# Attention in turns of three key tiles instead of two, with its slot plan laid anew, ahead of two MLPs on one core

## The chip, the core and the metric

The kernel runs on one core of a Trainium2 chip. The metric is the time of one execution on the device in microseconds (us), the median of several. The core has a matrix engine (TensorE, PE in the rows; its weight loads are PEld), a vector engine (DVE), a scalar engine (ACT), GpSimd (POOL) and a queue engine (SP) that issues most transfers. Each engine runs its own instructions strictly in the order in which the program issued them.

## The reference

Three layers, one after the other. The first is attention with B=2, H=8, S=768, D=64, in which a query sees only the keys of its own cluster:

```
q_assign = argmax(normalised q . normalised centroids)      # 16 clusters, k_assign alike
scores = where(q_assign == k_assign, q k^T / sqrt(D), -1e9)
attn = exp(scores - max(scores)); attn = attn / (sum(attn) + 1e-9)
x = (attn v) as [1536, 512]
```

The second is h = x w_in (512 to 2048), g = max(h, 0) + alpha min(h, 0), x = g w_out. The third is an RMS norm, then (silu(xn w_gate) * (xn w_val)) w_out with 1536 inner columns. Everything is float32.

## The kernel before

**Phases, slots and turns.** Heads are worked in eight pairs. A pair has two phases, one for each half of its queries (384 columns), so there are 16 phases, numbered 0 to 15. A phase has six slots, one for each key tile of 128 keys, which makes 96 slots. In a slot the two heads of the pair each get a score tile (`st_tile`, two matmuls L642 and L643 into one of three one-bank PSUM buffers `ps_st`; the exponential on ACT at L644 writes one half of a buffer `p`, of which there are four). Every second slot has a turn (`pv_tiles`): the exponentials of two key tiles against the values (L658, float32, two heads side by side in 64 columns of the array each) and against ones for the softmax's sums (L672, 32 columns each, four side by side), both into the two-bank buffer `ps_pv`. In phases 4 to 12 (`SUMMED`) DVE first adds the `p` of two tiles (L663), and only the last turn of the phase has sums, of the adds and of the last two tiles.

**Maxima.** A slot also holds one max tile (`max_tile`, two matmuls L595 into the one two-bank buffer `ps_mx`, reduced on DVE at L599), for a phase nine slots ahead (`LEAD`; phases 0 to 3 have slots of their own in `AHEAD`). When a head's three tiles are reduced, `max_split` (DVE L604, L605) cuts the maximum in two parts, `max_rows` (PE L620, into the single buffer `ps_pr`) turns them into rows, and `rows_copy` (ACT L629) puts these into the operand of the score matmuls.

**Ends of phases.** `out_evac` (ACT L680) takes sums and values out of `ps_pv`, `out_sums` (PE L687) and `out_recip` (DVE L692, L693) make the reciprocals, `out_bcast` (PE L701) spreads them, `out_mult` (DVE L707) multiplies, and `out_split` (ACT L715, POOL L718) cuts the result into the two parts that the first MLP reads. L687, L701, L620, the cluster products (L458, L469) and the transposed one-hot rows (L516) all share `ps_pr`.

**Work for later pairs.** Loads, squares (ACT L411), norms (DVE), high and low parts (ACT L548, DVE or POOL L556), cluster products, argmax and one-hot rows of the pairs ahead stand in the tables `PAIR`, `FOURTH`, `THIRD`, `SECOND`. From slot 70 on the packed weights of the first MLP are decoded (`decode_step`; the tables `EARLY` and `TAIL` place the steps).

**What sets the order.** `plan()` lists every such step with a slot and an order number within the slot; `slot()` issues the steps of a slot by that number. The number is all that decides what an engine does first:

```
def slot(self, s):
    for _, _, fn, a in sorted(self.ev.pop(s, []), key=lambda x: x[:2]):
        fn(*a)
```

Behind the last slots come the two MLPs, all of whose matmuls stand at L919.

## Time and profile before

| | |
|---|---|
| three runs | 857.28, 857.35, 857.57 us; median 857.35 |
| the profiled execution | 859.05 us, its span 857.3 us |
| granted TensorE clock over the span | 0.998 of full speed |
| instructions in the span | 11501 |

The span is what the profiler sees between the first and the last instruction; the profiled execution lies 1.7 us above the median. In the rows, L with a number is a line of the kernel, `out<-in` are buffers, and xN counts instructions. A float32 matmul leaves two records, so four value matmuls stand as x8. The end of a matmul is modelled and overlaps the start of the next, so paces are read from start to start.

### The profile page before, as it was taken

The page shows a single profiled execution, that of the slowest core. Times are in us where ns is not written, and L with a number is a line of the kernel's source. Part 1 is how long each engine was busy: PE and PEld are TensorE (multiplying, and loading weights), DVE is VectorE, ACT ScalarE, POOL GpSimd, SP SyncE. Part 2 cuts the span into 40 slices and gives each one's busy share as a digit, 9 for nine tenths or more (in the row PEclk, how much of TensorE's full clock was granted, in tenths as well). Part 3 has the DMA queues.
Part 4 walks back from the last instruction along what each step waited for, and adds up shares of the span by engine and source line. Part 5 has one row for each costly group of instructions (what it writes and reads, how often), then busy time and mean ns, then how long its engine had stood idle before and what let it go on. Part 6 is the DMA issues. An engine that isn't in the chain of part 4 may idle for free.

```text
span 857.3 us, 11501 instructions
## 1 busy us (share of the span) xinstructions
PE 835.6 (97%) x4310; PEld 632.4 (74%) x4310; DVE 596.7 (70%) x904; ACT 330.9 (39%) x636; POOL 376.2 (44%) x323
## 2 busy tenths in 40 slices
PE   8999999999999999999999999999999999999998
PEld 5555666666556688887788888778888888888886
DVE  7778687776767439999889786887645545555523
ACT  6636555655545333333334344533222212222210
POOL 3420211221004427878777664444546455555511
PEclk9999999999999999999999999999999999999999
DMA  8776447625632002222222211001122121121012
GB/s 204 193 213 168 99 129 197 124 74 129 138 99 99 25 1 73 99 74 99 75 74 74 74 50 49 24 26 34 66 74 65 58 74 53 71 74 50 1 49 99
DMA packets 23623, 74.02 MB, mean 86 GB/s; under 512 B 3600, under 2 KB 4752, under 8 KB 23568
## 3 DMA queue, kind: packets, MB, share of 16 engines
q1 hardware_dynamic: 23568, 73.29, 29.6%
q8 instruction: 34, 0.56, 0.3%
q14 instruction: 21, 0.17, 0.1%
HBM read 49.88 MB, written 3.15 MB: 62 GB/s over the span
## 4 chain that ended last, share of the span: by engine, by line
PE 72%; DVE 18%; issue 3%; ACT 2%; DMA 1%; POOL 1%; SPq 0%; DVEq 0%; ACTq 0%; POOLq 0%
PE ps_st L919 24%; PE ps_mx L919 10%; PE ps_pv L919 10%; PE ps_pv L658 7%; PE ps_pr L919 5%; PE ps_mx L595 4%; DVE mx L599 4%; DVE dec_a L898 3%; PE ps_pv L672 3%; PE ps_st L642 3%; PE ps_st L643 3%; DVE x L1026 2%; DVE dec_a L896 2%; PE ps_pr L701 1%; DVE dec_e L901 1%
## 5 line engine op out<-in xcount | busy, mean ns | idle before, releaser
L982 POOL TENSOR_TENSOR gl<-v,gh 128x512 fp32r<-128x512 f32 x68 | 93.5, 1375 | 104.0 <-ACT gh L981 102.6
L644 ACT ACTIVATE p<-ps_st 128x384 f32<-128x384 f32 x192 | 85.1, 494 | 105.6 <-PE ps_st L643 104.9
L599 DVE TENSOR_REDUCE mx<-ps_mx 128x1 f32<-128x768 f32 x92 | 87.7, 954 | 42.6 <-PE ps_mx L595 41.9
L981 ACT CAST gh<-v 128x512 fp32r<-128x512 f32 x68 | 42.3, 622 | 134.1 <-DVE v L978 79.9
L978 DVE TENSOR_TENSOR v<-ps_st,t 128x512 f32<-128x512 f32 x36 | 24.9, 691 | 85.5 <-PE ps_st L919 85.5
L718 POOL TENSOR_TENSOR x1l<-X,x1h 128x384 fp32r<-128x384 f32 x15 | 16.0, 1065 | 148.5 <-ACT x1h L715 111.6
L658 PE MATMUL ps_pv<-p,vnat 128*64 128x384 f32 x384 | 74.0, 507 | 0.2 <-DVE mx L599 0.2
L974 DVE SCALAR_TENSOR_TENSOR v<-v,alpha,t 128x512 f32<-128x512 f32 x45 | 46.7, 1037 | 30.9 <-ACT v L973 30.9
L919 PE MATMUL ps_st<-x1h,stage 128*128 128x512 f32 x272 | 67.8, 390 | 0.0
L642 PE MATMUL ps_st<-op 128*128 128x384 f32 x192 | 67.5, 351 | 0.3 <-ACT p L644 0.3
L898 DVE SCALAR_TENSOR_TENSOR dec_a<-raw,dec_a 128x512 uint32<-128x512 uint32 x66 | 66.1, 1001 | 2.3
L1026 DVE TENSOR_TENSOR x<-ps_mx,x 128x1024 f32<-128x1024 f32 x36 | 43.8, 1218 | 31.1 <-PE ps_mx L919 31.1
L643 PE MATMUL ps_st<-op 82*128 82x384 f32 x192 | 65.0, 339 | 0.1
L595 PE MATMUL ps_mx<-op 80*128 80x384 f32 x184 | 55.3, 382 | 8.5 <-DVE mx L599 7.4
L906 POOL TENSOR_TENSOR dec_a<-dec_a,woh 128x512 f32<-128x512 f32 x28 | 45.4, 1623 | 36.1 <-ACT woh L909 32.3
L919 PEld LDWEIGHTS ps_st<-x1h,stage 128*128 128x128 f32 x272 | 50.9, 188 | 10.6 <-ACT x1h L1068 0.2
L595 PEld LDWEIGHTS ps_mx<-op 80*128 80x128 f32 x184 | 27.9, 188 | 38.7 <-DVE mx L599 17.9
L919 PE MATMUL ps_st<-x1h,wvh 128*128 128x512 f32 x144 | 56.1, 390 | 0.0
L919 PE MATMUL ps_st<-x1h,wvl 128*128 128x512 f32 x144 | 56.1, 390 | 0.0
L919 PE MATMUL ps_st<-x1h,wih 128*128 128x512 f32 x132 | 51.7, 392 | 0.0
L919 PE MATMUL ps_st<-x1h,wil 128*128 128x512 f32 x132 | 51.5, 390 | 0.0
L901 DVE TENSOR_SCALAR dec_e<-dec_a 128x512 uint32<-128x512 uint32 x66 | 48.7, 737 | 2.2
(282 smaller groups left out, 1969.9 us busy)
## 6 DMA issues: line engine op xcount, KB each, us to landing
raw<-in_moe_w_out_dram SPq DMA_DIRECT2D x28, 512.0 KB, 3.5
op<-stage SPq DMA_DIRECT2D x32, 384.0 KB, 5.7
raw<-in_moe_w_in_dram SPq DMA_DIRECT2D x15, 512.0 KB, 3.6
raw<-in_moe_w_val_dram SPq DMA_DIRECT2D x12, 512.0 KB, 3.4
raw<-in_moe_w_gate_dram SPq DMA_DIRECT2D x12, 512.0 KB, 3.4
op<-stage SPq DMA_DIRECT2D x16, 288.0 KB, 5.8
raw<-in_qt_dram SPq DMA_DIRECT2D x8, 384.0 KB, 4.5
raw<-in_kt_dram SPq DMA_DIRECT2D x8, 384.0 KB, 5.4
```

Of the source, the lines that this page charges most:

```text
L595: nc.tensor.matmul(ps[:, g, :self.HS], lhsT=o1[0:80, 0, t * 128:(t + 1) * 128], rhs=o1[0:80, 1, sl], start=True, stop=True)
L599: nc.vector.tensor_reduce(out=self.mx[ph][:, k:k + 1], in_=ps[:, :, :self.HS], op=ALU.max, axis=AX.XY)
L642: nc.tensor.matmul(ps, lhsT=o1[:, 1, ks], rhs=o1[:, 0, qs], start=True, stop=False)
L643: nc.tensor.matmul(ps, lhsT=o2[:, 1, ks], rhs=o2[:, 0, qs], start=False, stop=True)
L644: nc.scalar.activation(out=self.P[s][:, e], in_=ps, func=AF.Exp, scale=self.scale)
L658: nc.tensor.matmul(ps[64 * e:64 * e + 64], lhsT=self.vnat[ph // 2][:, e, t0 + y], rhs=P[y][:, e], start=t0 + y == 0, stop=t0 + y == T - 1)
L898: v.scalar_tensor_tensor(out=a, in0=top, scalar=0xC0000000, in1=a, op0=ALU.bitwise_and, op1=ALU.bitwise_or)
L901: v.tensor_scalar(out=e, in0=a, scalar1=0xFF800000, scalar2=None, op0=ALU.bitwise_and)
L919: self.nc.tensor.matmul(ps, lhsT=a, rhs=b, start=first and i == 0, stop=last and i == len(terms) - 1)
L974: nc.vector.scalar_tensor_tensor(out=v, in0=v, scalar=self.nalpha[:, a], in1=t, op0=ALU.mult, op1=ALU.add)
L982: nc.gpsimd.tensor_tensor(out=lo, in0=v, in1=f(hi), op=ALU.subtract)
L1026: nc.vector.tensor_tensor(out=dst, in0=ps, in1=dst, op=ALU.add)
```

## The change

A turn now takes three key tiles, and there are two of them in a phase, in the third and the sixth slot, in the same slot as their last key tile (before: three turns of two tiles, each in the slot after). The values' matmuls stay twelve a phase. The sums are now made in each turn: in the phases of `SUMMED` four matmuls, of the sum of the first two tiles (one add a turn, in a function of its own, `pv_add`) and of the third; in phases 0 to 3 and 13 to 15 six, four for the first two tiles and two for the third.

The max tile of the second slot of each phase now goes to `ps_pv` instead of `ps_mx` (the argument `aside`); the order number of a max tile follows from its slot modulo 3. Phases 2 and 3 have other slots for their max tiles, and `max_rows` and `rows_copy` of later phases come one slot later. The ends of phases come earlier: from phase 2 on the evacuation at the end of the phase's last slot, then `out_sums` in the next, `out_bcast` two and `out_split` three slots behind that slot (before: eight, ten and twelve slots behind the phase's first). The pairs' table is laid anew. The weights' decode is cut into seven steps of one instruction, with ACT's copy moved ahead of two of DVE's, and its steps have new places.

```
-            for t in range(T):
...
-                if t % 2:
-                    at(b + t + 1, 2, self.pv_tiles, (b + t) // 2)
-            calm = STEADY <= b + 7 and not last
-            at(b + (7 if calm else 6), 1.03 if calm else 3, self.out_evac, ph)
-            at(b + (7 if last else 8), -0.5 if last else 1.7, self.out_sums, ph)
-            at(b + (8 if last else 10), -0.3 if last else 2.2, self.out_bcast, ph)
+                if t % 3 == 2:
+                    if ph in SUMMED:
+                        at(b + t, 0.9, self.pv_add, b + t - 2)
+                    at(b + t, 2, self.pv_tiles, b + t - 2)
+            at(b + 5, 2.9, self.out_evac, ph)
+            x, y, z = (7, 8, 8) if last else (8, 10, 12) if ph < 2 else (6, 8, 9)
+            at(b + x, -0.5 if last else 1.7, self.out_sums, ph)
+            at(b + y, -0.3 if last else 2.2, self.out_bcast, ph)
...
-                early = s < 0 or s % 2 and (s > 15 or ph < DIRECT and (s == 15 or slots.count(s) > 1))
-                at(s, 2.7 if s in slots[:k] else 0.5 if early else 1.5 if s < STEADY else 1.01, self.max_tile, ph, k)
+                second = s in slots[:k]
+                o = 2.7 if second else 0.5 if s < 0 else (0.5, 1.01, 1.03)[s % 3]
+                if s >= 0 and s % 3 == 0 and s - 1 in DOUBLE:
+                    o = 1.03
+                aside = not k % 2 if s < 0 else s % T == 1 and not second
+                at(s, o, self.max_tile, ph, k, aside)
...
-                at(end, 1.45 if end % 2 and end > 0 else 1.6, self.max_split, ph, 1)
+                at(end, 2.75 if end == slots[-2] else 1.6, self.max_split, ph, 1)
                 at(end + 1, 0.7, self.max_rows, ph, 1)
...
-                at(end + 1, 0.7, self.max_rows, ph, None)
-                at(end + 1, 1.03, self.rows_copy, ph)
+                at(end + 2, 1.7, self.max_rows, ph, None)
+                at(end + 2, 1.71, self.rows_copy, ph)
...
+    def pv_add(self, s):
+        a = self.pre([128, 2, self.HS], f"add{s % self.T // 3}")
+        self.adds[s] = a
+        self.nc.vector.tensor_tensor(out=a, in0=self.P[s], in1=self.P[s + 1], op=ALU.add)
...
+        def total(q, y, start, stop):
+            r = 32 * (2 * e + y)
+            nc.tensor.matmul(sm[r:r + 32], lhsT=self.ones[:, 0:32], rhs=q[:, e], start=start, stop=stop)
+        if ph in SUMMED:
+            for e in range(2):
+                for y, q in enumerate((self.adds[s], P[2])):
+                    total(q, y, t0 == 0, t0 > 0)
+            del self.adds[s]
+            return
+        y0 = t0 // 3
+        for part in ((0, 1), (2,)):
+            for e in range(2):
+                for y in part:
+                    total(P[y], (y0 + y) % 2, t0 == 0 and y < 2, t0 > 0 and y > 0)
...
-    2: (7, 7, 8, 9, 9, 10),
-    3: (11, 11, 12, 13, 14, 15),
+    2: (7, 7, 8, 8, 9, 10),
+    3: (11, 11, 12, 13, 14, 14),
 }
+DOUBLE = (2, 8, 11, 14)
...
-        return [word, tail, lambda: nc.scalar.copy(out=hi, in_=af), rest]
+        return [
+            lambda: v.tensor_scalar(out=a, in0=top, scalar1=3, scalar2=0x3FFFFFFF,
...
+            lambda: nc.scalar.copy(out=hi, in_=af),
...
```

Three places show how PE's order moves. The first is the turn of phase 1 around slot 8 (PE; `ps_mx` is the max tile, `ps_st` a score tile). Before:

```order
L642 MATMUL ps_st<-op_1_119 128x384
L643 MATMUL ps_st<-op_1_123 128x384
L595 MATMUL ps_mx<-op_2_120 128x384 x2
L687 MATMUL ps_pr<-sel,ssb 128x2 x3
L658 MATMUL ps_pv<-p,vnat 64x384 x4
L672 MATMUL ps_pv<-p,ones 32x384 x4
L595 MATMUL ps_mx<-op_3_121 128x384 x2
```

And with the change:

```order
L667 MATMUL ps_st<-op_1_119 128x384
L668 MATMUL ps_st<-op_1_123 128x384
L620 MATMUL ps_mx<-op_2_120 128x384 x2
L719 MATMUL ps_pr<-sel,ssb 128x2 x3
L688 MATMUL ps_pv<-p,vnat 64x384 x6
L693 MATMUL ps_pv<-p,ones 32x384 x6
L620 MATMUL ps_mx<-op_3_121 128x384 x2
```

The turn has six matmuls of values and six of sums where it had four and four.

The second place is the step from slot 10 to slot 11 (PE; L701, later L733, is `out_bcast`, and L620, later L645, is `max_rows`, both into `ps_pr`). Before:

```order
L643 MATMUL ps_st<-op_1_123 128x384
L595 MATMUL ps_mx<-op_3_121 128x384 x2
L658 MATMUL ps_pv<-p,vnat 64x384 x4
L672 MATMUL ps_pv<-p,ones 32x384 x4
L701 MATMUL ps_pr<-idf,rs 64x128 x6
L595 MATMUL ps_mx<-op_2_120 128x384 x2
L620 MATMUL ps_pr<-idr,mh_130 64x128 x3
```

And with the change:

```order
L620 MATMUL ps_mx<-op_3_121 128x384 x2
L667 MATMUL ps_st<-op_1_119 128x384
L668 MATMUL ps_st<-op_1_123 128x384
L733 MATMUL ps_pr<-idf,rs 64x128 x6
L645 MATMUL ps_pr<-idr,mh_130 64x128 x3
L667 MATMUL ps_st<-op_0_118 128x384
L668 MATMUL ps_st<-op_0_122 128x384
```

The turn between the max tile and the broadcast is gone from there, and so is the max tile between the broadcast and `max_rows`.

The third place is the step from slot 14 to slot 15 (PE, same names). Before:

```order
L672 MATMUL ps_pv<-p,ones 32x384 x4
L595 MATMUL ps_mx<-op_3_121 128x384 x2
L642 MATMUL ps_st<-op_2_120 128x384
L643 MATMUL ps_st<-op_2_124 128x384
L642 MATMUL ps_st<-op_3_121 128x384
L643 MATMUL ps_st<-op_3_125 128x384
L595 MATMUL ps_mx<-op_0_118 128x384 x2
L620 MATMUL ps_pr<-idr,mh_131 64x128 x3
```

And with the change:

```order
L719 MATMUL ps_pr<-sel,ssb 128x2 x3
L688 MATMUL ps_pv<-p,vnat 64x384 x6
L693 MATMUL ps_pv<-p,ones 32x384 x6
L620 MATMUL ps_mx<-op_3_121 128x384 x2
L645 MATMUL ps_pr<-idr,mh_131 64x128 x3
L667 MATMUL ps_st<-op_2_120 128x384
L668 MATMUL ps_st<-op_2_124 128x384
```

`max_rows` of the fourth phase's second head now stands right behind that head's last max tile, where two score tiles and another max tile stood between.

## Rows read from the trace of the kernel before

**Rows 1.** The page, part 1: busy time and instructions of each engine.

```profile
PE 835.6 (97%) x4310; PEld 632.4 (74%) x4310; DVE 596.7 (70%) x904; ACT 330.9 (39%) x636; POOL 376.2 (44%) x323
```

**Rows 2.** Stretches: from:to, length, busy PE, PEld, DVE, ACT, POOL (instructions); PEclk, DMA share, GB/s.

```profile
216.00:262.00 46.00, 42.10 (x288) 26.24 (x284) 34.49 (x57) 21.45 (x51) 5.31 (x5) 1.00 0.47 118
300.00:350.00 50.00, 50.00 (x222) 41.40 (x222) 35.31 (x39) 17.56 (x31) 27.13 (x19) 1.00 0.14 45
```

**Rows 3.** Waits of PE in 20 to 80, 80 to 216, 216 to 262: total, times, longest.

```profile
PE ps_mx L595 <- DVE mx L599: 2.1, 7, 0.3
...
PE ps_mx L595 <- DVE mx L599: 1.6, 4, 0.5
...
PE ps_mx L595 <- DVE mx L599: 3.8, 4, 1.1
```

**Rows 4.** PE's timeline, 200 to 210 us: start, duration, engine, line, operation.

```profile
200.23 1.51 PE L658 MATMUL ps_pv<-p,vnat 128*64 128x384 f32 x8
201.57 0.82 PE L701 MATMUL ps_pr<-idf,rs 128*64 128x128 f32 x12
...
204.48 0.34 PE L642 MATMUL ps_st<-op 128*128 128x384 f32 x1
204.66 0.34 PE L643 MATMUL ps_st<-op 82*128 82x384 f32 x1
204.93 1.51 PE L658 MATMUL ps_pv<-p,vnat 128*64 128x384 f32 x8
206.37 0.85 PE L672 MATMUL ps_pv<-add,ones 128*32 128x384 f32 x8
207.04 0.83 PE L672 MATMUL ps_pv<-p,ones 128*32 128x384 f32 x8
207.80 0.61 PE L595 MATMUL ps_mx<-op 80*128 80x384 f32 x2
208.25 0.34 PE L642 MATMUL ps_st<-op 128*128 128x384 f32 x1
...
209.46 0.62 PE L595 MATMUL ps_mx<-op 80*128 80x384 f32 x2
```

**Rows 5.** PE's timeline around slot 5 and in slot 11.

```profile
33.17 1.51 PE L658 MATMUL ps_pv<-p,vnat 128*64 128x384 f32 x8
...
35.40 0.40 PE L620 MATMUL ps_pr<-idr,mh 128*64 128x128 f32 x3
...
37.16 0.46 PE L516 MATMUL ps_pr<-idr,oh 128*128 128x128 f32 x3 [0.61 <-ACT op L629]
...
57.55 0.39 PE L620 MATMUL ps_pr<-idr,mh 128*64 128x128 f32 x3 [0.19 <-DVE X L707]
```

**Rows 6.** ACT's timeline around slot 5.

```profile
35.77 0.85 ACT L411 ACTIVATE nat<-nat 128x768 f32<-128x768 f32 x1 [0.17 <-DMA nat<-in_kn_dram]
```

**Rows 7.** DVE's timeline, slots 10 and 11, and one max tile later.

```profile
54.17 0.95 DVE L599 TENSOR_REDUCE mx<-ps_mx 128x1 f32<-128x768 f32 x1
...
55.56 0.96 DVE L556 TENSOR_TENSOR stage<-raw,stage 128x768 fp32r<-128x768 f32 x1
...
56.94 0.56 DVE L707 TENSOR_TENSOR X<-ps_pr,osb 128x384 f32<-128x384 f32 x1 [0.42 <-PE ps_pr L701]
...
208.45 0.96 DVE L599 TENSOR_REDUCE mx<-ps_mx 128x1 f32<-128x768 f32 x1 [2.81 <-PE ps_mx L595]
```

**Rows 8.** ACT's timeline, 235 us: one of the decode's copies.

```profile
235.36 0.62 ACT L909 CAST stage<-nat 128x512 fp32r<-128x512 f32 x1
```

**Rows 9.** PE's timeline, 46 to 50 us.

```profile
46.07 2.83 PE L658 MATMUL ps_pv<-p,vnat 128*64 128x384 f32 x8
48.83 1.08 PE L672 MATMUL ps_pv<-p,ones 128*32 128x384 f32 x8
49.84 0.62 PE L595 MATMUL ps_mx<-op 80*128 80x384 f32 x2
```

**Rows 10.** Stretches, 47 to 48 us: columns as in rows 2.

```profile
47.00:48.00 1.00, 1.00 (x4) 0.23 (x3) 0.96 (x3) 0.00 (x0) 0.00 (x0) 0.50 0.83 227
```

More of the change, by code (lines that the diff above doesn't have):

```diff
@@ L24 @@
     "sq": ((-35, 4), (-34, 4)),
-    "ss": ((-34, 5), (-33, 5)),
-    "norm": tuple((t, 5 + n / 100) for n, t in enumerate([-32] + [-31] * 6 + [-30] * 7)),
+    "ss": ((-33, 5), (-32, 5)),
+    "norm": ((-30, 0.6), (-30, 0.61), (-29, 1.015), (-29, 1.016), (-29, 1.017))
+            + tuple((-28, 1.9 + n / 1000) for n in range(9)),
     "hi": ((-28, 1.06), (-27, 1.06)),
-    "lo": ((-26, 4.5), (-22, 4.5)),
-    "sims": ((-30, 1.6), (-29, 1.7)),
-    "scale": ((-29, 1.75),),
-    "arg": ((-27, 5), (-26, 5), (-25, 5), (-23, 5), (-21, 5)),
-    "oht": ((-19, 1.7),),
+    "lo": ((-25, 1.9), (-21, 1.06)),
+    "sims": ((-29, 1.7), (-27, 1.7)),
+    "scale": ((-27, 1.75),),
+    "arg": ((-25, 1.95), (-24, 1.6), (-23, 1.6), (-22, 1.9), (-22, 1.95)),
+    "oht": ((-21, 1.7),),
     "load_v": ((-9, 6),),
@@ L41 @@
     "hi": ((-24, 4), (-23, 4)),
-    "lo": ((-22, 2.1), (-20, 2.1)),
+    "lo": ((-22, 2.1), (-19, 2.1)),
     "sims": ((-24, 0.3), (-24, 1.7)),
@@ L88 @@
     (70, 2.45),
-    (71, -1),
-    (72, 9),
-    (73, 2.55),
-    (74, 9),
-    (75, 9),
-    (76, 9),
-    (77, 2.55),
-    (78, 9),
+    (71, 1.9),
+    (71, 1.91),
+    (72, 0.6),
+    (72, 0.61),
+    (73, 1.015),
+    (74, 1.9),
+    (74, 1.91),
+    (75, 0.6),
+    (76, 1.015),
+    (76, 1.016),
+    (77, 1.9),
+    (77, 1.91),
+    (77, 1.92),
+    (78, 0.6),
 )
 TAIL = (
-    (-15, 1.45, "decode_step"),
-    (-14, 9, "decode_step"),
-    (-13, 0.5, "decode_step"),
-    (-13, 9, "decode_step"),
@@ L120 @@
-    (-3, 9, "decode_step"),
-    (-2, 0.5, "decode_step"),
-    (-2, 9, "decode_step"),
+    (-14, 1.015, "decode_step"),
+    (-13, 1.9, "decode_step"),
+    (-13, 1.91, "decode_step"),
+    (-13, 1.92, "decode_step"),
+    (-12, 0.6, "decode_step"),
+    (-11, 1.015, "decode_step"),
+    (-10, 1.9, "decode_step"),
+    (-10, 1.91, "decode_step"),
+    (-9, 1.5, "decode_step"),
+    (-9, 1.51, "decode_step"),
+    (-9, 1.52, "decode_step"),
+    (-8, 1.5, "decode_step"),
+    (-8, 1.51, "decode_step"),
@@ new lines @@
+    (-8, 1.52, "decode_step"),
+    (-8, 1.53, "decode_step"),
+    (-7, 1.9, "decode_step"),
+    (-7, 1.91, "decode_step"),
+    (-7, 1.92, "decode_step"),
+    (-7, 1.93, "decode_step"),
+    (-6, 1.5, "decode_step"),
+    (-6, 1.51, "decode_step"),
+    (-6, 1.52, "decode_step"),
+    (-6, 1.53, "decode_step"),
+    (-5, 1.5, "decode_step"),
+    (-5, 1.51, "decode_step"),
+    (-5, 1.52, "decode_step"),
+    (-5, 1.53, "decode_step"),
+    (-4, 1.5, "decode_step"),
+    (-4, 1.51, "decode_step"),
@@ L123 @@
+    (-4, 1.52, "decode_step"),
+    (-4, 1.53, "decode_step"),
+    (-3, 1.5, "decode_step"),
+    (-3, 1.51, "decode_step"),
+    (-3, 1.52, "decode_step"),
+    (-3, 1.53, "decode_step"),
+    (-2, 1.5, "decode_step"),
+    (-2, 1.51, "decode_step"),
+    (-2, 1.52, "decode_step"),
+    (-2, 1.53, "decode_step"),
+    (-1, 1.9, "decode_step"),
+    (-1, 1.91, "decode_step"),
+    (-1, 1.92, "decode_step"),
     (-9, 2.55, "up_part", 0, 0),
@@ L592, in max_tile @@
         t = ph % 2 * X + x
-        ps = self.bk.pv() if not (k % 2 or ph) or (ph, k) == (1, 1) else self.bk.mx()
+        ps = self.bk.pv() if aside else self.bk.mx()
         for g, sl in self.halves():
@@ L653, in pv_tiles @@
         ps, sm = self.pv[ph][:, 0, :self.HS], self.pv[ph][:, 1, :self.HS]
-        P = [self.P.pop(2 * u + y) for y in range(2)]
-        how = dict(start=t0 == 0, stop=t0 == T - 2)
-        for y in range(2):
+        P = [self.P.pop(s + y) for y in range(3)]
+        for y in range(3):
             for e in range(2):
@@ L659, in pv_tiles @@
                                  start=t0 + y == 0, stop=t0 + y == T - 1)
-        if ph in SUMMED and t0 < T - 2:
-            a = self.pre([128, 2, self.HS], f"add{t0 // 2}")
-            self.adds.append(a)
-            nc.vector.tensor_tensor(out=a, in0=P[0], in1=P[1], op=ALU.add)
+        def total(q, y, start, stop):
[6 more added lines that the diff above has]
+            del self.adds[s]
             return
-        rounds = [self.adds, P] if ph in SUMMED else [P]
-        for x, q in enumerate(rounds):
-            if ph in SUMMED:
-                how = dict(start=x == 0, stop=x == 1)
+        y0 = t0 // 3
+        for part in ((0, 1), (2,)):
             for e in range(2):
-                for y in range(2):
-                    r = 32 * (2 * e + y)
-                    nc.tensor.matmul(sm[r:r + 32], lhsT=self.ones[:, 0:32], rhs=q[y][:, e], **how)
-        self.adds = []
+                for y in part:
+                    total(P[y], (y0 + y) % 2, t0 == 0 and y < 2, t0 > 0 and y > 0)
     def out_evac(self, ph):
@@ L1138, in decode_next @@
     def decode_next(self):
-        for step in range(4):
+        for step in range(7):
             self.decode_step()
```

56 lines of the change are left out of this document (18 added, 38 removed).

## Prediction, made before the change was run

> **What bounds the kernel now.** I read the busy times first. PE is busy for 97% of the span, DVE for 70% [rows 1], so what counts is the length of PE's own program and the places where it stands still. By stretches, the MLPs leave no gap: 50.00 of 50 us busy, while in the last part of the attention PE is busy for 42.10 of 46 [rows 2]. Whatever the change does is therefore decided before about 300 us.
>
> The waits say what PE stands still for: the reduction of the maxima at L599, which frees the one max buffer, 2.1 us in the early part, 1.6 in the middle, 3.8 in the last part [rows 3]. These are only the waits that show as idle PE; the end of a matmul is modelled, so I also compared each start with the one before at the paces below. By that count PE starts late by about 9.3 us from 20 to 80 us (some 21 places), 5.4 from 80 to 216 (1.5 in each two phases) and 5.7 from 216 to 262 (seven places).
>
> The paces come from one stretch without waits [rows 4]. A full matmul of 384 columns takes .18 (204.48 to 204.66), so a score tile or a max tile takes .35. Going from a full matmul into the values takes .27 (204.66 to 204.93), .09 above the pace. Values of two tiles take 1.34 (200.23 to 201.57, same tiling before and behind); with the change of width to the sums they take 1.44 (204.93 to 206.37), so the change of width costs .10. A round of four sums takes .67 (206.37 to 207.04); followed by a full matmul .76 (207.04 to 207.80), again .09 more, and the max tile that follows takes .45 (207.80 to 208.25) where .35 would do. One visit to the narrow tilings thus costs .09 + .09 + .10, about .29, beside its work.
>
> **The change, term by term.**
>
> *PE's program.* Narrow groups: before there are 48 turns, one broadcast that stands alone and one group of cluster products alone, 50; after, 32 turns, three broadcasts and six groups of products alone, 41. Nine fewer at .29 give −2.6. Changes of width: 30 from values to sums, 6 from sums to a broadcast and 5 from sums to products before, 32 and 13 after; four more at .10 give +.4. The values' matmuls and, in phases 4 to 12, the sums (two rounds of four a phase before and after) keep their number. In the other seven phases three rounds of four become two of four and two of two. What a round of two costs no row of before shows: at least half a round (.33), at most a whole one (.67). I take the whole: two groups of 64 columns take .67 a tile in the values and four groups of 32 take .67 a round [rows 4], so the time goes with the passes, not with the groups that share them. Seven phases with one more round at .65 give +4.5 (the lower end 0). Together **+2.3**.
>
> The Trainium skill, "TensorE: Matmul & The Clock Gate", section "Measured speedup vs the span model", says that packed tiles take the span of about one matmul whatever their number, plus some 4 ns for each. By it the term is the same +4.5 and the total 859.6; pricing the columns in use would make it 0 and the total 855.1. No run shown has a half-empty round of 32 columns.
>
> *Early part, slots 0 to 18.* Here a turn used to stand where work had time to finish. (a) Slot 5: the one-hot product waits for ACT's row copy. Before, PE had a turn from 33.17 to 35.40 ahead of `max_rows` and then still waited .61 [rows 5]. ACT's square of the next keys starts only when its transfer lands at 35.77 and holds the copy up by .85 [rows 6]. With the turn behind it, PE arrives earlier and stands longer: some 2.3 late instead of .94, +1.4. (b) Slot 11: `max_rows` shares its buffer with the broadcast, so `out_mult` must be done. On DVE a reduction, two small operations, a low part and `out_mult` stand in a row: 54.17, 55.56, 56.94 to 57.50; `max_rows` starts at 57.55 [rows 5, 7]. Before, a turn lay between the max tile and the broadcast; now DVE's 3.3 us (.65 to the reduction's start as at 207.80 and 208.45 [rows 4, 7], 1.39 to the low part, .96, .56, less waits) run against .45 + .35 + .8 of PE: 2.5 late instead of .4, +2.2. (c) Slot 15: `max_rows` right behind its own last max tile must wait for the reduction and the split, .65 + 1.39 less the .45 of the tile [rows 4, 7]: +1.6. (d) Slot 13, the same with two score tiles and a max tile in between: +.8. (e) Max tiles closer than the 1.66 that the buffer needs (207.80 to 209.46 [rows 4]): +.4. Gone are several waits of .2 to .5, 2.2 together, part of the 2.1 for L599 [rows 3]. Sum **+4.2**; bounds: none of these new waits (−2.2) and all of them with a further .5 at each (+6.5).
>
> *Middle, slots 24 to 66.* The waits for L599 (1.6 idle [rows 3], 1.5 late in each two phases) lose their cause, since every sixth max tile has another bank. New are a score buffer that waits for ACT in the sixth slot, where a high part and an output part stand ahead of an exponential (about .6), and `max_rows` behind the copy of one-hot rows (.45). 1.1 instead of 1.5 in each of some four pairs of phases: **−1.5**; bounds −5.4 (all gone) and +1.
>
> *Last part, slots 69 to 86.* Decode steps of one instruction let reductions go between, so most of the 3.8 us for L599 [rows 3] go. What I expect to stay is 2.9 of 5.7: 1.7 in slot 76, where the decode's copy (.62 on ACT [rows 8]) now stands ahead of an exponential and of `rows_copy` and itself waits for two DVE operations, and three or four of .25 to .45. **−2.8**; bounds −5.7 and 0.
>
> *MLPs and transfers.* PE is saturated there [rows 2], its order is the same, and the decode's seven steps are called where four were: 0. The early ends of phases move ACT and DVE work that is far from PE's path: 0; without that cover the output parts (`out_split`) would hold the first MLP, which starts three slots later.
>
> Sum: 2.3 + 4.2 − 1.5 − 2.8 = +2.2. The profiled execution would take 859.05 + 2.2 = 861.25; it lies 1.7 above the median, which the change should not alter, so the forecast is 857.35 + 2.2 = **859.6**. 0.2%, about what a measurement of this kernel can tell from no change, is 1.7 us: the boundaries are 855.6 and 859.1.
>
> **The rivals.**
>
> *Half rounds* (10%). A round of two sums costs half of one of four. It decides below about .36. The term of 4.5 falls to 0: 855.1. For it speaks only that no row excludes it; against it that two groups cost as much a pass as four [rows 4].
>
> *No new waits* (22%), on the other side: the plan was laid so that ACT and DVE arrive in time, and the waits that I derive for slots 11, 15 and 76 and the middle do not come. Mechanism: what decides is whether DVE reaches the reduction at once (in before it does at 208.45, .65 behind the tile [rows 7]) and whether ACT is free. If about 6.1 of the new waits fall away, 859.6 − 6.1 = 853.5. It decides from a rest of some 4 us of such waits on (2.2 + 1.7 less). For it: the page's DVE is 30% idle. Against: on the orders that I read, the waiting operation stands directly behind its cause.
>
> *The clock stays up* (12%). At 46 us the granted clock is .50, that is 1.2 GHz of 2.4 [rows 10], and values of two tiles take 2.76 (46.07 to 48.83) instead of 1.44, the sums 1.01 (48.83 to 49.84) instead of .76 [rows 9]; about 1.6 lost, behind PE's waits of the early part. If the new order has no such fall, 858.0.
>
> *More falls* (18%). The new waits in slots 5, 11 and 15 are each longer than most that PE had; if the clock falls behind two more of them, at 1.6 each, 862.8.
>
> The remaining 38% are the forecast, with 856.4 to 862.5 as its own range.
>
> **How the numbers follow.** Faster than 855.6: most of the second rival (.20), half of the first (.06) and the low edges of forecast and clock (.04), .30. Slower than 859.1: the forecast's upper part (.22), more falls (.17) and some of the clock's case (.03) make .42; the rest is .28. The range 852.0 to 864.0 reaches from the second rival with a little of the others' gain on top to more falls with 1.2 of new waits, and leaves out some 2 in 10.
>
> **What would show it.** Right: the turns of phases 0 to 3 and 13 to 15 last 1.93 to 2.1 of values and 1.3 of sums, and a round of two takes as long as one of four; the waits in slots 5, 11 and 15 for ACT's row copy, `out_mult` and L605 stand at PE with 1.5 to 2.5 each; the idle of PE from 216 to 262 is about half of before; the MLPs' paces are unchanged. Wrong: a sums turn of some 1.0 (half rounds); PE busy for over 57 of the 60 us from 20 to 80 (no new waits); or a difference behind 300 us, which none of my terms allows.

## The result: 1.4% slower, and most of it is TensorE's clock

| | median us | lowest to highest, runs | granted clock of the runs |
|---|---|---|---|
| before | 857.46 | 857.28 to 859.15, 4 | profiled one 0.998 |
| changed | 870.39 | 867.60 to 870.55, 4 | 0.988 (three), 0.992 (the profiled one) |
| changed, on another chip | 866.48 | 864.27 to 868.80, 4 | 0.990 to 0.996 |

The ratio of the first two is 1.0139, with a 95% interval of 1.0115 to 1.0163; on the other chip (run `e13_changed` below) it is 1.0102, 1.0080 to 1.0123. The forecast was 859.6 with a range to 864.0: the sign was right, the size was not.

The page of the changed kernel, part 1, and the clock's line of part 2 (each digit is a fortieth of the span, in tenths of full speed):

```profile
PE 841.0 (97%) x4310; PEld 638.1 (74%) x4310; DVE 603.8 (70%) x904; ACT 333.1 (38%) x636; POOL 375.1 (43%) x323
PEclk9988999999999999999999999999999999999999
```

PE has as many instructions as before and is as busy [rows 1]; the third and fourth digit are new. The stretches of the changed kernel (columns as in rows 2) show where:

```profile
48.00:51.00 3.00, 3.00 (x14) 0.94 (x14) 1.17 (x4) 0.00 (x0) 0.00 (x0) 0.50 0.89 222
...
61.50:64.50 3.00, 3.00 (x12) 0.96 (x8) 0.50 (x1) 0.33 (x1) 0.00 (x0) 0.50 1.05 300
...
82.00:88.50 6.50, 6.50 (x28) 4.49 (x30) 5.14 (x8) 1.47 (x3) 0.00 (x0) 0.50 0.00 0
90.00:216.00 126.00, 123.90 (x847) 80.44 (x839) 101.64 (x204) 74.07 (x160) 24.29 (x18) 1.00 0.56 134
216.00:262.00 46.00, 45.35 (x301) 29.26 (x303) 32.47 (x53) 23.71 (x54) 3.04 (x3) 1.00 0.41 99
300.00:350.00 50.00, 50.00 (x233) 41.21 (x232) 31.28 (x37) 17.57 (x32) 22.07 (x16) 1.00 0.10 32
```

These are three falls, stretches at 0.50 (1.2 GHz of 2.4), where the profiled execution of before had one [rows 10]. In stretches of half a microsecond they add up to 13.7 us at half clock, which costs half of that, 6.8, as an estimate; the one fall of before, 3.4 us long, cost 1.7, which is also what its profiled execution lay above the median. Without them the two profiled executions would have taken 867.60 − 6.8 = 860.8 and 859.05 − 1.7 = 857.35. So the change costs **3.4 us at full clock**, and the clock the rest: 5.1 more than in the profiled execution of before, and some 10 in the three slower runs at 0.988 (a loss of 0.012 of a span of 868.5).

In these two executions, by the start of a slot's first score matmul: the changed kernel is 1.6 us behind at slot 3, 12.5 at slot 27 (7.4 without the falls), 12.0 at slot 69, 9.0 at slot 87 and 8.5 at the end. Not all of such a shift is loss: at the start of a phase's fourth slot, as slots 3, 27, 69 and 87 are, the changed kernel already has a tile of values and a round of sums behind it that the kernel before does later, at least some 1.3 us (an estimate from the paces in [rows 4]), and at the end this is gone. So the loss falls in the early part, and the last part gives some of it back, less than the 3.5 by which the shift shrinks from slot 69 to the end. PE is busy for 45.35 us there from 216 to 262, where it was busy for 42.10 [rows 2].

PE's timeline of the changed kernel in the early part, the instructions that waited and the values' matmuls (L688) behind them:

```profile
37.76 0.45 PE L541 MATMUL ps_pr<-idr,oh 128*128 128x128 f32 x3 [0.81 <-ACT op L654]
...
46.04 0.62 PE L620 MATMUL ps_mx<-op 80*128 80x384 f32 x2 [0.96 <-DVE mx L624]
...
47.15 3.71 PE L688 MATMUL ps_pv<-p,vnat 128*64 128x384 f32 x12
...
59.50 0.39 PE L645 MATMUL ps_pr<-idr,mh 128*64 128x128 f32 x3 [2.10 <-DVE X L739]
...
61.14 3.85 PE L688 MATMUL ps_pv<-p,vnat 128*64 128x384 f32 x12
...
71.50 0.39 PE L645 MATMUL ps_pr<-idr,mh 128*64 128x128 f32 x3 [1.10 <-DVE sims L510]
...
73.50 2.17 PE L688 MATMUL ps_pv<-p,vnat 128*64 128x384 f32 x12
...
79.19 0.37 PE L645 MATMUL ps_pr<-idr,mh 128*64 128x128 f32 x3 [1.54 <-DVE mh L630]
...
81.71 1.01 PE L620 MATMUL ps_mx<-op 80*128 80x384 f32 x2 [0.70 <-DVE mx L624]
```

The waits are those of slots 5, 8, 11, 13, 15 and 16. The same turn of three tiles takes 2.17 behind one of them and 3.7 to 3.9 behind two others, where the clock is at half.

### The profile page after: what moved, and what is told of

Its sections match the earlier page's. It is cut to its first block, busy times and chain, and to the rows that moved or that the text cites. A ratio compares the mean times of both kernels' runs of the same rounds, so it can differ in the third digit from the quotient of the medians.

```text
span 865.8 us, 11504 instructions
## 1 busy us (share of the span) xinstructions
PE 841.0 (97%) x4310; PEld 638.1 (74%) x4310; DVE 603.8 (70%) x904; ACT 333.1 (38%) x636; POOL 375.1 (43%) x323
## 4 chain that ended last, share of the span: by engine, by line
PE 74%; DVE 16%; ACT 4%; issue 3%; POOL 1%; ACTq 0%; DVEq 0%; POOLq 0%
PE ps_st L954 24%; PE ps_mx L954 10%; PE ps_pv L954 9%; PE ps_pv L688 8%; PE ps_pr L954 5%; PE ps_pv L693 4%; DVE dec_a L937 4%; PE ps_mx L620 3%; PE ps_st L667 3%; PE ps_st L668 3%; DVE x L1061 2%; DVE mx L624 2%; DVE dec_a L935 2%; PE ps_pr L733 1%; DVE dec_e L940 1%
## 5 line engine op out<-in xcount | busy, mean ns | idle before, releaser
L624 DVE TENSOR_REDUCE mx<-ps_mx 128x1 f32<-128x768 f32 x78 | 74.4, 954 | 38.3 <-PE ps_mx L620 37.6
L688 PE MATMUL ps_pv<-p,vnat 128*64 128x384 f32 x384 | 74.9, 519 | 1.4 <-ACT p L669 1.1
L667 PE MATMUL ps_st<-op 128*128 128x384 f32 x192 | 69.7, 363 | 0.9 <-ACT p L669 0.9
L937 DVE SCALAR_TENSOR_TENSOR dec_a<-raw,dec_a 128x512 uint32<-128x512 uint32 x66 | 68.0, 1030 | 2.2
L688 PEld LDWEIGHTS ps_pv<-p,vnat 128*64 128x64 f32 x384 | 27.3, 141 | 33.8 <-issue 27.1
L941 DVE SCALAR_TENSOR_TENSOR dec_e<-raw,dec_e 128x512 f32<-128x512 uint32 x66 | 46.6, 707 | 2.2
```

The source lines that it names most:

```text
L624: nc.vector.tensor_reduce(out=self.mx[ph][:, k:k + 1], in_=ps[:, :, :self.HS], op=ALU.max, axis=AX.XY)
L667: nc.tensor.matmul(ps, lhsT=o1[:, 1, ks], rhs=o1[:, 0, qs], start=True, stop=False)
L688: nc.tensor.matmul(ps[64 * e:64 * e + 64], lhsT=self.vnat[ph // 2][:, e, t0 + y], rhs=P[y][:, e], start=t0 + y == 0, stop=t0 + y == T - 1)
L937: lambda: v.scalar_tensor_tensor(out=a, in0=top, scalar=0xC0000000, in1=a, op0=ALU.bitwise_and, op1=ALU.bitwise_or),
L941: lambda: v.scalar_tensor_tensor(out=ef, in0=bot, scalar=2.0 ** -52, in1=ef, op0=ALU.mult, op1=ALU.mult),
```

## The experiments

The theory: the new waits make PE stand still in the early part, and the clock then falls. The main rival: the longer turns of narrow float32 matmuls make it fall, whatever waits there are. The runs e1 to e4 shared a chip, and so did e5 to e8, e9 to e12 and e13 to e16, each four with the kernel before, whose median was 857.35 to 857.58 every time, mostly at a granted clock of 1.0.

**The early waits shortened** (`e1_rows_late`, on the changed kernel):

```
-    "lo": ((-16, 2.1), (-14, 2.1)),
+    "lo": ((-16, 2.1), (-14, 2.3)),
-    "oht": ((-13, 1.7),),
+    "oht": ((-13, 2.6),),
-                at(mid + 1 if ph else mid + 2, 1.8 if ph else 0.6, self.max_rows, ph, 0)
+                at(*((14, 0.7) if ph == 3 else (mid + 1, 1.8) if ph else (mid + 2, 0.6)), self.max_rows, ph, 0)
-                at(end + 1, 0.7, self.max_rows, ph, 1)
+                at(*{2: (11, 1.9), 3: (16, 0.7)}.get(ph, (end + 1, 0.7)), self.max_rows, ph, 1)
```

> The changed kernel, with the row matmuls of the maxima in slots 11, 13 and 15 moved to where their input is ready (slot 11 behind the score tiles, the start of slot 14, the start of slot 16), the third pair's one-hot product behind the turn of slot 11, and one low part behind out_mult. PE's work is the same. Theory (the new waits make PE stand still and the clock falls behind each long one): the waits of 2.10, 1.10 and 1.54 us go for the most part (3 to 4.5 us), and with them the falls at 61 and 82 us (1.7 and 3.4 us): 870.4 becomes 860 to 863, granted clock 0.996 to 0.998. Rival (the falls come from the longer turns, which are float32 in narrow tiles): only the waits go, 866 to 867, the clock stays at 0.988 to 0.992.

Measured: 860.75 (858.55 to 865.15, 6 runs), ratio 1.0043 (1.0023 to 1.0062), clock 1.0 in one run, 0.997 in four, 0.992 in one. As the theory has it. The one run at 1.0 took 858.55, 2.3 less than the 860.8 above: that is about what the moved waits cost by themselves. The wait of slot 13 did not go (1.09, still for L510).

**Dummies in the waits** (`e2_warm`, on the changed kernel; `warm` is the program's own helper, a matmul on zeros):

```
+        for t, o, n in ((8, 1.025, 3), (11, 0.65, 8), (13, 1.7, 4), (15, 0.65, 6), (16, 1.005, 2)):
+            at(t, o, self.warm, n, self.bk.st)
```

> The changed kernel with 23 dummy matmuls of 512 columns on zeros put directly ahead of the five instructions that wait in slots 8, 11, 13, 15 and 16 (3, 8, 4, 6 and 2 of them, 5.2 us of matmul at full clock). The waits' causes stay, only PE is not idle in them. Theory (idle PE lowers the clock): the falls behind slots 11 and 15 go, 870.4 becomes 861 to 865 although work was added. Rival (the turns do it): falls stay, 870 to 873.

Measured: 861.41 (861.04 to 861.63, 4 runs), clock 1.0 in all four. The stretch from 20 to 90 us (columns as in rows 2) of this kernel, of the changed one, and of before:

```profile
20.00:90.00 70.00, 65.31 (x411) 41.39 (x410) 50.47 (x107) 35.33 (x73) 14.76 (x38) 1.00 0.68 179
```

```profile
20.00:90.00 70.00, 59.84 (x347) 35.65 (x350) 46.79 (x92) 31.33 (x63) 13.76 (x37) 0.90 0.66 168
```

```profile
20.00:90.00 70.00, 65.53 (x411) 37.44 (x410) 54.31 (x118) 36.15 (x74) 16.56 (x39) 0.98 0.68 179
```

With 23 useless matmuls and the same turns the kernel is 9.0 us faster than the changed kernel's median on the first chip and 5.1 faster than on the other, and its executions lie within 0.6 us. That is the theory's case and not the rival's. The changed kernel itself did not run on this chip, but its eight executions on two other chips all had falls, and so had the four of `e3_carry` below, which ran on this chip with all the waits. It is also the changed kernel at full clock, seen directly: 861.4, of which some 0.6 us are the dummies themselves, by the difference to 860.8.

**The third tile's sums carried to the second turn** (`e3_carry`, on the changed kernel):

```
-        y0 = t0 // 3
-        for part in ((0, 1), (2,)):
+        if t0 == 0:
+            self.kept = P[2]
+        for x, part in enumerate([P[:2]] if t0 == 0 else [[self.kept, P[0]], P[1:]]):
             for e in range(2):
-                for y in part:
-                    total(P[y], (y0 + y) % 2, t0 == 0 and y < 2, t0 > 0 and y > 0)
+                for y, q in enumerate(part):
+                    total(q, y, t0 == 0, t0 > 0 and x == 1)
```

> The changed kernel, in whose phases 0 to 3 and 13 to 15 the third tile's sums are carried to the phase's second turn: two tiles' sums in the first turn, four tiles' in the second, three rounds of four column groups where there were two of four and two of two. If a half round costs a whole one: seven rounds of 0.65 less, 870.4 becomes about 866 with the waits as they are (in the early part some of the gain of the first turns is eaten by the waits behind them: 866 to 868). If a half round costs half: no change, 870. If the length of the turns brings the falls of the clock, 2 to 5 us more are gained.

Measured: 860.60 (859.65 to 862.20, 4 runs), ratio 1.0039 (1.0024 to 1.0054), clock 0.992 to 0.996. The profiled execution, 859.65, had 6.8 us at half clock, so 856.2 without: 4.6 less than the changed kernel, seven rounds of 0.65. PE's timeline says the same by itself. The changed kernel, slot 2, six matmuls (x12):

```profile
28.67 1.49 PE L693 MATMUL ps_pv<-p,ones 128*32 128x384 f32 x12
30.09 0.62 PE L620 MATMUL ps_mx<-op 80*128 80x384 f32 x2
```

And this one, slot 2 with four matmuls (x8) and slot 5 with eight (x16):

```profile
28.75 0.85 PE L693 MATMUL ps_pv<-p,ones 128*32 128x384 f32 x8
29.53 0.62 PE L620 MATMUL ps_mx<-op 80*128 80x384 f32 x2
...
39.66 1.50 PE L693 MATMUL ps_pv<-p,ones 128*32 128x384 f32 x16
41.09 0.44 PE L667 MATMUL ps_st<-op 128*128 128x384 f32 x1
```

Four take 0.78, six take 1.42 and eight take 1.43: a round of two column groups costs a whole one, and the rival of half rounds is out. All the waits were kept, and its clock, 0.992 to 0.996, lies above that of the changed kernel on the first chip (0.988 to 0.992) but not above that on the other (0.990 to 0.996); so it does not tell whether the shorter turns made fewer falls.

**One wait in the kernel before** (`e4_before_wait`):

```
-                at(end, 1.45 if end % 2 and end > 0 else 1.6, self.max_split, ph, 1)
-                at(end + 1, 0.7, self.max_rows, ph, 1)
+                at(end, 0.52 if ph == 3 else 1.45 if end % 2 and end > 0 else 1.6, self.max_split, ph, 1)
+                at(*((15, 0.55) if ph == 3 else (end + 1, 0.7)), self.max_rows, ph, 1)
```

> The kernel before, with one row matmul of phase 3 moved from slot 16 to directly behind its last max tile in slot 15, as the changed kernel has it: one wait of about 1.6 us for the reduction and the split, nothing else. Theory: PE stands still once more and the clock falls behind it; 857.4 becomes 859 to 862.5 (1.6 for the wait and 0 to 3.4 for a fall at about 70 to 75 us). Rival (turns make the falls): 858.5 to 859, clock 0.998 as before.

Measured: 858.84 (858.42 to 861.60, 5 runs), ratio 1.0030 (1.0015 to 1.0046). The wait is there in the trace:

```profile
71.02 0.38 PE L620 MATMUL ps_pr<-idr,mh 128*64 128x128 f32 x3 [1.55 <-DVE mh L605]
```

Three runs at 0.999 to 1.0 took 858.4 to 858.8, so the wait costs 1.2; two runs at 0.996 took 861.2 and 861.6. Of ten runs of the kernel before beside them nine had 1.0 and one 0.999, and none of its 47 runs beside the sixteen experiments lies under 0.997. One wait thus brought falls in some of the executions, not in all.

**Longer turns in the kernel before** (`e7_before_long`):

```
-        rounds = [self.adds, P] if ph in SUMMED else [P]
+        rounds = [self.adds, P] if ph in SUMMED else [P, P] if t0 == 0 and ph < 4 else [P]
...
+            elif len(rounds) == 2:
+                how = dict(start=True, stop=x == 0)
```

> The kernel before with one more round of sums (four matmuls, written over by the true ones) in the first turn of phases 0 to 3: these turns then last as long as the changed kernel's (some 2.7 us), no wait is added. Theory (idle PE lowers the clock): 4 rounds at 0.65 = 2.6 more less what they cover of waits, 858.5 to 860, clock 0.998 to 1.0. Rival (long turns lower the clock): falls as in the changed kernel, 862 or more, clock 0.996 or lower.

Measured: 860.12 (859.63 to 861.68, 6 runs), clock 0.997 to 1.0, beside 0.997 to 1.0 for 17 runs of before. It costs its four rounds, 2.3 to 2.8. Two of its six executions stand at 0.998 or less, as do three of the 17 of before, so the clock nearly stays: the rival's strong form, that turns of this length alone bring the falls of the changed kernel, is out.

**One wait filled at a time** (`e9_warm15`, `e10_warm11` on one chip, `e14_warm8` on the chip of `e13_changed`). The edits are single entries of the list of `e2_warm`:

```
+        for t, o, n in ((15, 0.65, 6), (16, 1.005, 2)):
...
+        for t, o, n in ((11, 0.65, 8),):
...
+        for t, o, n in ((8, 1.025, 3),):
```

> The changed kernel with dummy matmuls only ahead of the two waits of slots 15 and 16 (6 and 2). Theory (each fall follows an idle stretch of PE): the long fall that began at 82 us goes, those at 48 and 61 us stay: 870.4 less 3.4 to 6, 864 to 867, clock 0.992 to 0.996. Rival (the sum of low activity over the whole early part counts, whatever the place): no change or a change as large as with all five places.

> The changed kernel with dummy matmuls only ahead of the wait of slot 11 (8). Theory: the fall at 61 us goes, those at 48 and 82 us stay: 870.4 less 1.7 to 3, 867 to 869. Rival as for the run before: no change, or a gain as large as with all five places.

> The changed kernel with 3 dummy matmuls ahead of the wait of slot 8 alone. If a fall hangs on the idle stretch right ahead of it: the fall at 48 us goes, those at 61 and 82 us stay, 1.7 less than the changed kernel on this chip. If all idle stretches of the early part count together: a gain of 3 or more, falls at other places too go. If it is chance: no difference.

Measured: 864.26 (863.58 to 866.31), clock 0.994 to 0.996; 863.66 (862.31 to 865.06), clock 0.996 to 0.998; 868.25 (864.97 to 869.48), clock 0.988 to 0.996; four runs each. In their profiled executions, `e9_warm15` had falls at 47 and 61 us and none behind, as the theory has it. `e10_warm11` is a miss: with slot 11 filled the fall at 48 us, ahead of it, was absent as well, and its only fall began at 70 us. `e14_warm8` had falls at 59 and 73 us and is no better than the changed kernel beside it (866.48); on the chip of the other two the changed kernel did not run. Single fills can't assign a fall to a wait, because the falls move between executions of one kernel:

> The changed kernel itself, beside the three others on one chip. If the number of falls is the kernel's: 867 to 871 at a clock of 0.988 to 0.992. If it is the chip's: 862 to 866 at 0.994 to 0.998, and the comparison with the runs on other chips holds only for the part that the clock does not explain.

Measured as in the table: 866.48, four runs with clocks from 0.990 to 0.996. That lies between the two cases: the falls vary both between chips and between executions on one chip, so a gain against a run on another chip is sure only as far as it exceeds this spread. The stretches of its profiled execution:

```profile
60.00:63.00 3.00, 3.00 (x12) 0.85 (x8) 0.29 (x1) 0.13 (x1) 0.00 (x0) 0.50 1.03 277
81.00:83.00 2.00, 2.00 (x15) 1.27 (x13) 1.13 (x3) 0.49 (x1) 0.00 (x0) 0.50 0.00 0
90.00:300.00 210.00, 206.78 (x1372) 134.19 (x1371) 160.61 (x295) 114.95 (x252) 46.80 (x35) 1.00 0.46 114
```

Here the fall at 48 us is missing and that at 82 us is half as long: 6.8 us at half clock, 3.4 lost, and 864.27 − 3.4 = 860.9. The price at full clock agrees with the first trace to 0.1 us; the falls are what varies.

**The decode alone** (`e6_before_decode`: the kernel before with the changed kernel's `EARLY`, the decode entries of `TAIL` and the seven steps; `e15_old_decode`: the changed kernel with those of before). The first, cut:

```
-    (71, -1),
+    (71, 1.9),
+    (71, 1.91),
...
-        return [word, tail, lambda: nc.scalar.copy(out=hi, in_=af), rest]
...
-        for step in range(4):
+        for step in range(7):
```

> The kernel before with only the weights' decode of the changed kernel: seven steps of one instruction, the copy ahead of two of DVE's operations, and its places. If the finer steps are what takes PE's waits away between 216 and 262 us: 3 to 5 us less there, 852.5 to 854.5. If the waits go because turns of three leave more time between max tiles: no change, 856.5 to 858, or slower, since the places were not chosen for turns of two.

> The changed kernel with the decode of the kernel before: four steps, the copy behind two more of DVE's operations, the old places. In the kernel before the new decode alone gave 3.7. If the new decode is what helps: 3 to 5 us slower than the changed kernel, with PE's waits for the reductions back from 225 us on. If turns of three had taken the waits away by themselves: within 1 us.

Measured: `e6_before_decode` 853.66 (853.52 to 853.83, 4 runs), ratio 0.9951 (0.9935 to 0.9968), clock 1.0 throughout: 3.7 us gained by this part alone. The stretch from 213 to 300 us of it, and of before:

```profile
213.00:300.00 87.00, 86.39 (x548) 56.18 (x547) 58.62 (x91) 39.79 (x89) 24.68 (x19) 1.00 0.32 89
```

```profile
213.00:300.00 87.00, 83.10 (x537) 53.57 (x536) 57.50 (x90) 40.96 (x92) 23.99 (x19) 1.00 0.33 89
```

`e15_old_decode` took 873.52 (872.80 to 874.49, 4 runs) at 0.988 to 0.990. Its profiled execution, 874.20, loses 10.2 to the clock, in falls of 3.4, 6.8 and 10.2 us at half clock, of which this stretch lies in the last:

```profile
83.00:92.50 9.50, 9.49 (x38) 5.50 (x42) 6.31 (x9) 1.47 (x3) 0.00 (x0) 0.50 0.12 32
```

The 864.0 left is 3.1 more than the changed kernel beside it (860.9). PE's waits from 225 us on:

```profile
PE ps_pv L664 <- ACT p L645: 2.4, 1, 2.4
PE ps_mx L596 <- DVE mx L600: 1.8, 2, 1.3
PE ps_pv L664 <- DVE mx L600: 0.9, 3, 0.4
```

The gain in the last part is the new decode's, with turns of either length; its finer steps, the moved copy and the new places were exchanged together, so which of them gives it is not shown.

**Without the second bank** (`e16_no_aside`, on the changed kernel):

```
-                aside = not k % 2 if s < 0 else s % T == 1 and not second
+                aside = not k % 2 if s < 0 else False
```

> The changed kernel with every max tile from slot 0 on in the one max bank. If the bank aside is what keeps the middle free of waits for the reductions: 0.3 to 0.6 us more in each phase, some 4 to 8 us slower in all. If the spacing of the max tiles suffices: within 1 us.

Measured: 878.94 (869.82 to 879.13, 4 runs), ratio 1.0221 (1.0171 to 1.0270), clock 0.982 in three runs, 0.993 in one. The stretch from 20 to 100 us, and PE's waits for the reductions from 20 to 80 us:

```profile
20.00:100.00 80.00, 68.86 (x356) 39.35 (x355) 47.52 (x93) 31.77 (x64) 13.68 (x37) 0.81 0.60 154
```

```profile
PE ps_mx L620 <- DVE mx L624: 4.5, 9, 1.1
```

Those waits were 2.6 in the changed kernel. The execution loses 15.4 us to the clock; 863.6 without, 2.8 more than the changed kernel. Without the falls it is 0.6 us behind the changed kernel at slot 24 and 2.8 at slot 87: most of the price is paid behind 100 us, though no wait for a reduction shows there as idle. In the middle, every twelve slots, one max tile starts 0.17 us later behind the score tile and the values another 0.11 later behind it, so 0.28 is lost. PE's timeline in slot 50 of this kernel, and of the changed one:

```profile
184.22 0.33 PE L668 MATMUL ps_st<-op 82*128 82x384 f32 x1
184.56 0.62 PE L620 MATMUL ps_mx<-op 80*128 80x384 f32 x2
185.12 1.19 PE L688 MATMUL ps_pv<-p,vnat 128*64 128x384 f32 x6
```

```profile
174.52 0.34 PE L668 MATMUL ps_st<-op 82*128 82x384 f32 x1
174.69 0.51 PE L620 MATMUL ps_mx<-op 80*128 80x384 f32 x2
175.14 1.19 PE L688 MATMUL ps_pv<-p,vnat 128*64 128x384 f32 x6
```

So the place expected was right and the size too large: 2.8 in all instead of 4 to 8, some 0.14 a phase in the middle. The larger part of the measured difference is the clock. It goes the theory's way: 1.9 us more of waits for the reductions in the early part (the wait in slot 13 was 0.6 shorter), and 8.5 us more lost to the clock than in the first trace of the changed kernel, 12.0 more than in the one beside it.

**Towards a better kernel** (`e5_rows_carry`: `e1_rows_late` and `e3_carry` together; `e8_more`: three more moves; `e11_more_warm`: dummies in the waits that are left). The edits of `e8_more` beyond `e5_rows_carry`, and that of `e11_more_warm`:

```
-    "scale": ((-17, 1.2),),
+    "scale": ((-17, 2.75),),
...
+                at(mid, 1.8 if ph == 3 else 1.6, self.max_split, ph, 0)
...
+                at(*((14, 1.035) if ph == 3 else (mid + 1, 1.8) if ph else (mid + 2, 0.6)), self.max_rows, ph, 0)
...
+            at(b + x, -0.5 if last else 2.65 if ph == 1 else 1.7, self.out_sums, ph)
...
+        for t, o, n in ((5, 1.69, 3), (8, 1.025, 2), (9, 1.025, 2), (12, 0.25, 1), (15, 1.025, 1), (16, 1.005, 2)):
+            at(t, o, self.warm, n, self.bk.st)
```

> The changed kernel with both edits at once: the row matmuls of slots 11, 13 and 15 later, and the third tile's sums carried to the second turn. Without any fall of the clock the first alone gave 858.55 and the second saves 4.2; if they add up, 854 to 855 where the clock stays up and 856 to 858 with one fall of 3 to 4 us at half clock. If the shorter first turns leave less cover and the early waits grow by what is saved there, 856 to 857 at a clock of 1.0.

> As the kernel with both edits, and three more moves against waits of PE: the third pair's scaling behind the second max tile of slot 7 (wait of 0.96 in slot 8 becomes 0.5), the fourth pair's scaling ahead of the split on DVE with the rows behind the max tile of slot 14 (wait of 1.09 becomes 0 to 0.3), the sums of phase 1 behind the turn. 1 to 1.5 us less than that kernel, and fewer falls of the clock: 853 to 854.5 at a clock of 1.0.

> The kernel with all five moves (852.55 where the clock stayed up, up to 856.6 where it fell) and 11 dummy matmuls in the waits that are left, in slots 5, 8, 9, 12, 15 and 16. Theory: no more falls, every execution near 852.6 to 853.5, the spread under 1 us. Rival (falls come from elsewhere): spread as before, 852.5 to 857.

Measured: 855.82 (853.96 to 858.71, 10 runs, clock 0.994 to 1.0); 854.31 (852.55 to 856.64, 6 runs, clock 0.996 to 1.0); 852.89 (852.71 to 853.40, 4 runs, clock 0.999 to 1.0). The last, at a ratio of 0.9943 (0.9928 to 0.9958), beats both kernels. It has the same order of work as `e8_more` and eleven useless matmuls more; its median is 1.4 us lower and its spread 0.7 instead of 4.1, though the two ran on different chips and two of the six executions of `e8_more` stayed at 1.0 without them.

**The early part as before, the rest as changed** (`e12_hybrid`: `pv_tiles` of two tiles, the old places and the old rule for max tiles' order in slots up to 19, the old evacuation for phases 0 to 3; everything else as changed, with `e3_carry`). Cut:

```
+                if ph < DIRECT:
+                    if t % 2:
+                        at(b + t + 1, 2, self.pv_pair, b + t - 1)
+                elif t % 3 == 2:
```

> Phases 0 to 3 as before (turns of two tiles, the old places of maxima, rows and ends of phases), all else as changed (turns of three with the sums carried in phases 13 to 15, the bank aside, the new tables, the decode in seven steps). If the loss lies in slots 0 to 18 alone: the early part is as before (857.4, clock 1.0), the middle about 0.5 less, the last part 3.5 less and 2 less for the carried sums: 851 to 852.5, better than every kernel so far. If the middle's and the last part's gains need the early plan: 854 or more.

Measured: 858.14 (857.72 to 859.31, 10 runs), ratio 1.0006 (0.9997 to 1.0015), clock 1.0 in nine. A miss, and the trace says why: the seam of the two plans waits. PE's timeline there, and the stretch behind 90 us:

```profile
78.61 0.62 PE L620 MATMUL ps_mx<-op 80*128 80x384 f32 x2 [0.68 <-DVE mx L624]
90.74 0.62 PE L620 MATMUL ps_mx<-op 80*128 80x384 f32 x2 [1.27 <-DVE mx L624]
97.23 0.62 PE L620 MATMUL ps_mx<-op 80*128 80x384 f32 x2 [0.84 <-DVE mx L624]
101.75 0.62 PE L620 MATMUL ps_pv<-op 80*128 80x384 f32 x2 [0.43 <-ACT osb L729]
111.35 0.88 PE L750 MATMUL ps_pr<-idf,rs 128*64 128x128 f32 x12 [1.36 <-ACT op L654]
```

```profile
90.00:150.00 60.00, 56.20 (x386) 36.73 (x386) 44.34 (x85) 33.78 (x74) 9.59 (x8) 1.00 0.61 152
```

4.6 us of waits that neither parent has there. Through slot 18 the kernel is level with the kernel before, so the loss of the changed kernel does lie in the early part. The waits explain 4.6 of the some 6 us by which the expectation missed; the 3.5 that it took for the last part were too much, as said of the shifts above. They also limit the theory: PE stood 1.27 and 1.36 us here, and the clock did not fall.

## Why the prediction was wrong

**At full clock the sum was near.** It gave +2.2; at full clock the change costs 3.4 (860.8 against 857.35, from two executions), inside the forecast's own range of 856.4 to 862.5. That it came so near is partly luck: the middle gave about 1 less than forecast and the decode about 0.9 more.

- *PE's program, +2.3.* Its uncertain part, 4.5 for the half-empty rounds, measured 4.6 (`e3_carry`). The price of a visit to the narrow tilings was summed too low: the .10 read on the max tile behind it is left out, and with it nine fewer visits give −3.4 instead of −2.6. The Trainium skill, "TensorE: Matmul & The Clock Gate", section "Measured speedup vs the span model", has the span of packed tiles go with one tile's duration, plus a few ns for each further one; the runs agree (1.42 us for six matmuls, 1.43 for eight).
- *Early part, +4.2.* Slots 11 and 15 came as worked out: 2.10 idle for `out_mult` (2.5 late expected) and 1.54 for the split (1.6). Slot 13 waited 1.10 instead of 0.8, and for something else: not for the split but for L510, which reads the cluster products out of `ps_pr` and stood behind the split on DVE, whose first operation took 0.74 there. Slot 5 waited 0.81 (0.97 late), not 2.3. Slots 8 and 16, 0.96 and 0.70 for L624, I had only as 0.4 together. As an estimate, of the 7.4 by slot 27 some 1.3 is work done earlier and 2.6 the half-empty rounds of phases 0 to 3; 3.5 is left for the waits, less what fewer visits saved.

DVE's timeline around slot 13:

```profile
70.04 0.74 DVE L629 TENSOR_SCALAR mh<-mx 128x3 fp32r<-128x3 f32 x1
...
70.89 0.55 DVE L510 TENSOR_TENSOR sims<-ps_pr,n_a 128x384 f32<-128x384 f32 x1
```

- *Middle, −1.5.* Too large: from slot 27 to slot 69 the kernel gains 0.5 in all, work included. The waits for L599 went; waits of 0.38 in most phases (0.21 of it as idle) for ACT, for a score buffer or the one-hot rows' copy, came in their place.
- *Last part, −2.8.* Right in kind, too small: `e6_before_decode` shows 3.7 for the decode alone. The chain in slot 76 that I priced at 1.7 exists, but costs 0.63, because PE meets it in a turn. ACT's timeline, the decode's copy (L939) waiting for DVE and holding up the exponentials, and PE's wait:

```profile
243.05 0.62 ACT L939 CAST stage<-nat 128x512 fp32r<-128x512 f32 x1 [1.33 <-DVE nat L937]
243.58 0.48 ACT L669 ACTIVATE p<-ps_st 128x384 f32<-128x384 f32 x1
244.09 0.95 ACT L654 CAST op<-ps_pr 2x384 fp32r<-2x384 f32 x2
245.06 0.87 ACT L669 ACTIVATE p<-ps_st 128x384 f32<-128x384 f32 x2
```

```profile
245.60 0.92 PE L688 MATMUL ps_pv<-p,vnat 128*64 128x384 f32 x3 [0.63 <-ACT p L669]
```

- *MLPs, 0.* Right: the shift stays at 8.5 us from 294 us to the end.

**The step that failed is the clock.** Two places of the text carry it. The sentence that the profiled execution "lies 1.7 above the median, which the change should not alter" treated as an offset what was a fall: the median run of before has none, its profiled execution has one of 1.7. I had its price [rows 9, 10] and did not connect the two numbers; so the sum held no term for falls, and the 858.0 of *the clock stays up* took a fall off a median that has none. And the rival *more falls* had the mechanism and two of the places, slots 11 and 15, but the wrong size and chance: I gave two falls at 1.6 each and 18%. All eight executions of the changed kernel had at least 3.4 us lost to falls and the worst about 10, since falls of two and three times the length that I had seen occur (6.8 us at half clock in the first trace of the changed kernel and 10.2 in `e15_old_decode`, where the one of before had 3.4). The early part of the changed kernel has six waits of 0.70 to 2.10 us where the longest of before there was 0.61 [rows 5], in a part of the program that already had a fall now and then; the forecast should have had the falls as its likeliest case.

The other rivals: half rounds are out (`e3_carry`); *the clock stays up* did not happen to the changed kernel, but is what `e2_warm` makes of it, 861.4; *no new waits* failed in slots 11, 13 and 15 and held in the last part.

**What stays open.** That filling PE's waits takes the falls away is shown (`e2_warm`, and on other chips `e11_more_warm` beside `e8_more`), and that first turns of this length alone don't bring them (`e7_before_long`). The dummies use the array's full width, so no run separates that PE isn't idle from what it is filled with. Why idle PE matters so much before 100 us is not: the waits of 1.05 to 1.08 behind 216 us in the kernel before, those of `e12_hybrid` at 91 and 111 us and one of 2.4 in `e15_old_decode` left the clock at 1.00. In the early phases the turns have more rounds of sums than in phases 4 to 12; that long turns and waits must come together is a guess that no run here isolates. Nor is it shown why four executions of `e15_old_decode` stand at 0.988 to 0.990, where the changed kernel stands at 0.990 to 0.996 on the same chip: the two differ only from slot 59 on, and the falls of its trace end before slot 21. The Trainium skill, "TensorE: Matmul & The Clock Gate", section "Part 1: The HAM clock gate (the "warmup" mystery)", says that the activity monitor runs freely and does not start with the kernel, so that one kernel has different numbers of slow matmuls at its start from run to run. The runs here vary in the same way in mid-kernel: one kernel at 864.27 and 868.80 on one chip.

## What to carry to other kernels

Before the terms of a change are summed, look whether the profiled execution and the median run have the same granted clock: a difference of one fall, here 1.7 us, says that falls already occur, and a new wait in that part may then cost more than its length (the wait of 1.55 us in `e4_before_wait` cost 1.2 without falls and up to 4.1 with them). A short wait that can't be moved away is worth trying to fill with dummy matmuls, which here cost 0.2 to 0.6 us at full clock; the medians with them were 1.4 to 9 lower, across chips. And take a large replanning apart: the new decode alone gained 3.7 us, which the rest of the change gave away.
